# A fused gated linear attention and SiLU feed-forward: five masked scores split between ScalarE and VectorE, state updates spread over two engines, one pool for the inputs, and a new order of all work

## Chip, core and metric

The kernel runs on one core of one Trainium2 chip. The metric is the device time in microseconds (us) of one execution. Engines are named as in the profile: PE is TensorE (PEld its weight loads), DVE is VectorE, ACT is ScalarE, POOL is GpSimd, SP is SyncE, which only issues transfers here.

## What is computed

A recurrence over 768 positions for 4 x 8 heads of width 48, whose outputs go through a feed-forward block with SiLU (384 to 2048 to 384). Cut to what matters:

```python
f = 1.0 / (1.0 + np.exp(-f_logit))
for t in range(S):
    state = f[:, :, t, :, None] * state + np.einsum('bhd,bhe->bhde', k[:, :, t], v[:, :, t])
    y[:, :, t] = np.einsum('bhd,bhde->bhe', q[:, :, t], state)
x = y.transpose(0, 2, 1, 3).reshape(B * S, H * D)
h = x @ w_in
out = (h / (1.0 + np.exp(-h))) @ w_out
```

## The kernel before

The recurrence is computed in chunks of 128 positions. The logarithms of the gates are summed within a chunk by a matmul with a triangular matrix (`cs`); their exponentials `a` and `ia` scale q and k. Within a chunk the result is masked scores (q k^T, times a triangular mask) times v; across chunks a state of 48x48 per head is carried.

There are 24 chunks (4 batch rows, 6 chunks each), and the work goes by twelve pairs of chunks (`PAIRS`). Pairs 0 to 3 (form T) hold the first two chunks of one batch row, interleaved so that one load has both; pairs 4 to 11 (form N) hold the same chunk of two batch rows. A pair gives 256 columns for the feed-forward part.

Nothing schedules the work but a text, `PLAN`: one word per step, and every engine does its own steps in the order of the text. A word is `kind.pair.index:engine:buffers`; the engines are S (SP), A (ACT), V (DVE), G (POOL), P (PE). The steps, in the order of a chunk's life:

- `f`, `k`, `q`, `v`: loads. `E`, `L`: exponential and logarithm of the gate, on ACT. `cs`: the sum over the chunk, on PE. `a`, `ia`, `al`: exponentials of it, on ACT (`al` is the decay of a whole chunk).
- `qg`, `ki`: q and k times these, on DVE or POOL, into the tile `qk`. `tq` and `qkc`: transpose on PE and its copy, for pairs 0 to 3; `qkD`: the same as a transposing transfer on SP's queue, for the others.
- `sc`: scores on PE. `at`: scores from PSUM times the mask, on DVE, into `atm` (bf16). `vb`: v as bf16. `y`: masked scores times v, with the state's part (`yi` where that is a step of its own).
- `d`: k^T v on PE; `sd`: the state plus that; `su`: that times the decay, into the state `st`.
- `yc`, `yT`, `xc` (or `yD`, a transposing transfer): y as bf16, transposed, as input `xT` of the feed-forward part. `mi.P.j`: an eighth of its first product on PE (6 matmuls). `si`: SiLU on ACT. `mo.P.i.n`: a quarter of the second product for one chunk (4 matmuls). `oc`, `so`: copy and store of the result.
- `wi`, `wo`: a quarter each of w_in and w_out, by POOL's queue. `idle.C.N`: N matmuls of C columns whose result nobody reads; they keep PE working in the start.

Before, `at` is always one DVE instruction that reads PSUM:

```python
elif kind == "at":
    r = rest[2]
    mask = masks[i] if T else triu
    ENG[eng].tensor_mul(at("atm", P, i)[:, r], at(f"s{r}", P, i).rearrange("p (n c) -> p n c", c=C), mask[:, None, :].to_broadcast([C, NP, C]))
```

and `su` is always two POOL instructions, one for each half of the heads. Loads of f, k, q and v have buffers of their own (`SLOTS`: 4, 6, 6 and 6, of which the order uses 2, 2, 2 and 3), `E` writes into a buffer `e`. A step that needs a buffer waits until the last reader of the buffer's former content is done; what stands behind it on the same engine waits too.

Of the kernel before, what the change touches and what calls it, by code (L numbers as in the profile page):

```python
# [517 lines left out]
```

## Time and profile before

| what | value |
|---|---|
| median of three runs | 177.89 us (177.02 to 178.26) |
| the profiled execution | 177.35 us |
| its span, first to last instruction | 175.6 us |
| granted clock of PE | 1.0 |
| busy PE, ACT, DVE, POOL | 169.4, 129.8, 81.2, 61.2 us |
| DMA | 32.12 MB, 183 GB/s mean over the span |

The span is what the views of the profile show; 1.75 us of the profiled execution lie outside it. Rows of a view give an engine, the line of the kernel, the operation, output and inputs by tile name (`pb` is a PSUM bank of 512 fp32, `x` the exponentials, `qkTT` and `qkT` the transposed q and k), partitions x elements and type. In groups and in the timeline a matmul's duration includes the time it takes to drain, so that rows of PE overlap. A window's row has for each engine the busy time and the number of instructions, then PE's granted clock, the share of the DMA engines' time, and GB/s.

### The profile page before, as it was taken

Reading aid. Unit: us, or ns where it says so; the run is one execution under the profiler, and the core shown is the slowest. Engines: PE = TensorE matmul, PEld = TensorE weight load, DVE = VectorE, ACT = ScalarE, POOL = GpSimd, SP = SyncE. Lnnn points to the kernel's source line nnn. Section 1 sums busy time; section 2 is a strip of 40 time slices with the busy share of each in tenths; the row PEclk is TensorE's granted clock in tenths of the full one; section 3 lists DMA queues with packets and bytes.
Section 4 is the critical chain, followed back from the end, with each engine's and each line's share of the span. In section 5 each row is a group of like instructions: output and inputs, shape, how many; then the busy total and the mean of one; then the engine's idle time right before and its main releaser. Section 6 shows DMA issues by size and latency. Waiting matters only on the chain.

```text
span 175.6 us, 4754 instructions
## 1 busy us (share of the span) xinstructions
PE 169.4 (96%) x1927; PEld 125.2 (71%) x1930; DVE 81.2 (46%) x166; ACT 129.8 (74%) x239; POOL 61.2 (35%) x104
## 2 busy tenths in 40 slices
PE   6889999999999999999999999999999999999992
PEld 2446788666886788766787687686797676786872
DVE  7199760047786782125777165035770152520101
ACT  3968578952999989998489687999489575191630
POOL 6048393002473348400646324400461970000000
PEclk9999999999999999999999999999999999999999
DMA  5999999999998997999697797899967999223202
GB/s 146 320 325 265 211 216 201 188 182 240 232 172 164 210 208 158 228 183 217 128 230 166 143 236 158 205 188 231 225 128 183 193 191 230 54 61 118 90 4 90
DMA packets 110677, 32.12 MB, mean 183 GB/s; under 512 B 104096, under 2 KB 110528, under 8 KB 110656
## 3 DMA queue, kind: packets, MB, share of 16 engines
q1 hardware_dynamic: 106048, 27.76, 76.0%
q0 software_dynamic: 3936, 3.74, 11.9%
q10 hardware_dynamic: 672, 0.33, 0.6%
q8 instruction: 15, 0.25, 0.6%
q14 instruction: 6, 0.05, 0.1%
HBM read 25.17 MB, written 4.72 MB: 170 GB/s over the span
## 4 chain that ended last, share of the span: by engine, by line
PE 79%; ACT 11%; DVE 5%; DMA 2%; issue 2%
PE pb L286 35%; PE pb L249 29%; ACT x L317 3%; ACT hT L254 3%; PE pb L350 3%; ACT L485 2%; DVE qk L322 2%; DMA f<-in_f_logit_dram 2%; PE pb L362 2%; PE pb L366 2%; PE pb L346 1%; PE pb L312 1%; PE pb L383 1%; PE pb L374 1%; DVE atm L354 1%
## 5 line engine op out<-in xcount | busy, mean ns | idle before, releaser
L249 PE MATMUL pb<-xT,w_in_sb 128*128 128x256 bf16 x576 | 69.1, 272 | 0.3 <-ACT hT L254 0.2
L286 PE MATMUL pb<-w_out_sb,hT 128*128 128x384 bf16 (+2 forms) x400 | 68.6, 320 | 0.0
L249 PEld LDWEIGHTS <-w_in_sb 128*128 128x128 bf16 x576 | 54.8, 98 | 9.0 <-issue 0.8
L254 ACT ACTIVATE hT<-pb 128x512 bf16<-128x512 f32 x96 | 50.5, 611 | 10.9 <-PE pb L249 10.7
L286 PEld LDWEIGHTS <-hT 128*128 128x128 bf16 x400 | 37.2, 98 | 20.5 <-issue 0.2
L393 POOL TENSOR_TENSOR st<-sd,al 48x192 bf16<-48x192 f32 x40 | 21.4, 535 | 59.0 <-PE pb L362 33.4
L354 DVE TENSOR_TENSOR atm<-pb,triu 128x512 bf16<-128x512 f32 x32 | 20.1, 684 | 11.2 <-PE pb L350 6.6
L317 ACT ACTIVATE x<-pb 128x384 f32<-128x384 f32 x48 | 21.0, 501 | 5.4 <-PE pb L305 3.0
L485 ACT ACT_TABLE_LOAD x17 | 21.8, 1283 | 0.3
L184 DVE COPY ob<-pb 128x384 f32<-128x384 f32 (+1 forms) x11 | 5.7, 528 | 27.3 <-PE pb L286 27.3
L387 DVE TENSOR_TENSOR sd<-pb,st 128x384 f32<-128x384 f32 x16 | 8.8, 552 | 11.8 <-PE pb L383 10.3
L322 POOL TENSOR_TENSOR qk<-q,x 128x384 bf16<-128x384 f32 x11 | 10.9, 996 | 9.0 <-ACT x L317 6.1
L322 POOL TENSOR_TENSOR qk<-k,x 128x384 bf16<-128x384 f32 x11 | 11.8, 1081 | 5.7 <-ACT x L317 2.4
L182 ACT COPY ob<-pb 128x384 f32<-128x384 f32 (+1 forms) x14 | 6.7, 477 | 8.5 <-PE pb L286 8.1
L234 ACT ACTIVATE e<-f 128x768 f32<-128x768 f32 x12 | 10.1, 840 | 3.8 <-DMA f<-in_f_logit_dram 3.7
L322 DVE TENSOR_TENSOR qk<-q,x 128x384 bf16<-128x384 f32 x13 | 8.2, 648 | 7.2 <-ACT x L317 7.1
L354 DVE TENSOR_TENSOR atm<-pb,mask 128x512 bf16<-128x512 f32 x16 | 10.1, 684 | 1.6 <-issue 1.0
L436 PE MATMUL pb<-zero,triu 128*128 128x512 bf16 (+1 forms) x26 | 9.0, 449 | 1.4 <-POOL triu masks.py:66 1.4
L184 DVE CAST yb<-pb 128x384 bf16<-128x384 f32 x14 | 7.6, 554 | 5.1 <-PE pb L366 2.6
L184 DVE COPY qkTT<-pb 128x1024 bf16<-128x1024 bf16 x7 | 4.6, 683 | 11.0 <-PE pb L329 11.0
L322 DVE TENSOR_TENSOR qk<-k,x 128x384 bf16<-128x384 f32 x13 | 9.0, 707 | 1.0 <-DMA k<-in_k_dram 0.8
L184 POOL CAST vb<-v 128x384 bf16<-128x384 f32 x12 | 6.4, 535 | 8.0 <-DMA v<-in_v_dram 7.7
(71 smaller groups left out, 141.1 us busy)
## 6 DMA issues: line engine op xcount, KB each, us to landing
f<-in_f_logit_dram SPq DMA_DIRECT2D x11, 384.0 KB, 5.1
k<-in_k_dram SPq DMA_DIRECT2D x10, 384.0 KB, 5.5
q<-in_q_dram SPq DMA_DIRECT2D x10, 384.0 KB, 5.4
v<-in_v_dram SPq DMA_DIRECT2D x10, 384.0 KB, 4.9
out_dram<-ob SPq DMA_DIRECT2D x13, 192.0 KB, 2.1
w_in_sb<-in_moe_w_in_dram POOLq DMA_DIRECT2D x4, 384.0 KB, 8.6
w_out_sb<-in_moe_w_out_dram POOLq DMA_DIRECT2D x4, 384.0 KB, 10.5
out_dram<-ob SPq DMA_DIRECT2D x14, 96.0 KB, 3.3
```

What stands on the lines that cost most here:

```text
L184: ENG[eng].tensor_copy(dst, src)
L234: return nc.scalar.activation(e, at("f", P)[:, j * w:(j + 1) * w], AF.Exp, scale=-1.0)
L249: nc.tensor.matmul(h[:, i, cols], w_in_sb[:, kk, n * 128:(n + 1) * 128], at("xT", P)[:, kk, cols], start=(kk == 0), stop=(kk == KT - 1))
L254: return nc.scalar.activation(at("hT", P)[:, 2 * j:2 * j + 2, :], at("h", P, j).rearrange("p (n c) -> p n c", n=2), AF.Silu)
L286: nc.tensor.matmul(at("o" + key, P, i)[:, 0:cols.stop - cols.start], at("hT", P)[:, n, i * C:(i + 1) * C], w_out_sb[:, n, cols], start=(n ...
L317: nc.scalar.activation(at(kind, P, i).rearrange("p h d -> p (h d)"), at("cs", P, i)[:, 0:HD], AF.Exp, scale=1.0 if kind == "ia" else -1.0)
L322: ENG[eng].tensor_mul(at("qk", P, i)[:, j, :, 0:D], heads("qk"[j], P, i), at("ia" if j else "a", P, i))
L354: ENG[eng].tensor_mul(at("atm", P, i)[:, r], at(f"s{r}", P, i).rearrange("p (n c) -> p n c", c=C), mask[:, None, :].to_broadcast([C, NP, C]))
L387: nc.vector.tensor_add(at("sd", P, i), d_ps, prev_state(P, i))
L393: nc.gpsimd.tensor_mul(at("st", P, i)[lo:lo + D, :, r * D:(r + 1) * D], at("sd", P, i)[lo:lo + D, :, r * D:(r + 1) * D], al_of(P, i)[lo:lo ...
L436: nc.tensor.matmul(buf["pb", int(got)][:, 0:rest[0]], triu, zero[:, 0:rest[0]], start=True, stop=True, skip_group_check=True)
L485: nc.scalar.preload_act_table_set(turns[n])
```

## The change

1. Four masked scores of pairs 1 and 0 and one of pair 2 are split: ACT copies the scores from PSUM to `atm` as bf16 (`ax`), and DVE (or POOL, for pair 2) multiplies `atm` by the mask in place (`am`).
2. `su` may run on DVE: 12 of the 20 do, 8 stay on POOL.
3. f, k, q and v share one pool of input buffers (`inp`, of which the order uses 8), and `E` works in place.
4. The masks are built in fewer steps, partly on DVE; filler matmuls use the zero tile for both operands; the matmuls that give `al` its input (`on`) are a step of their own, which may follow later than `cs`.
5. `PLAN` is written anew from end to end. Among other things the second quarter of w_in (`wi.3`) is requested right behind the first (`wi.1`), and filler falls from 14080 to 10496 columns.

Otherwise the number of steps of each kind stays the same. By engine: `oc` on ACT 14 to 10 (DVE 11 to 15), `sd` on ACT 2 to 0, `vb` on ACT 6 to 9, `xc` on ACT 4 to 6, `qkc` on ACT 1 to 2; `ki` on POOL 11 to 14, `qg` on POOL 11 to 9.

```diff
-SLOTS = dict(f=4, k=6, q=6, v=6, e=2, lf=3, x=5, qk=5, vb=7, ...)
+SLOTS = dict(inp=24, lf=3, x=5, qk=5, vb=7, ...)
 PLAN = """
-f.1.0:S:0 f.1.1:A: E.1.0:A:0 L.1.0:A:0 idle.512.10::0 cs.1.1:P:0 f.0.0:S:1 E.0.0:A:1 k.1.0:S:0 L.0.0:A:1 idle.512.1::1 cs.1.0:P:1
+f.1.0:S:0 f.1.1:A: E.1.0:A: L.1.0:A:0 mk.0:G: mk.1:G: mv.0:V: idle.512.10::0 cs.1.0:P:0 f.0.0:S:1 E.0.0:A: idle.256.1::1 cs.1.1:P:1 k.1.0:S:2
...
+        if kind == "mv":
+            nc.vector.tensor_copy(tincl, triu)
+            for t in (tincl, tstrict):
+                nc.vector.memset(t[0:HC, HC:C], 0.0)
...
-            e = at("e", P)[:, j * w:(j + 1) * w]
+            e = at("f", P)[:, j * w:(j + 1) * w]
             if kind == "E":
-                return nc.scalar.activation(e, at("f", P)[:, j * w:(j + 1) * w], AF.Exp, scale=-1.0)
+                return nc.scalar.activation(e, e, AF.Exp, scale=-1.0)
...
+        elif kind == "ax":
+            nc.scalar.copy(at("atm", P, i)[:, rest[2]], at(f"s{rest[2]}", P, i).rearrange("p (n c) -> p n c", c=C))
+        elif kind == "am":
+            half = at("atm", P, i)[:, rest[2]]
+            ENG[eng].tensor_mul(half, half, (masks[i] if T else triu)[:, None, :].to_broadcast([C, NP, C]))
...
         elif kind == "su":
             for r in range(2):
                 lo = 64 * r
-                nc.gpsimd.tensor_mul(at("st", P, i)[lo:lo + D, :, r * D:(r + 1) * D], at("sd", P, i)[lo:lo + D, :, r * D:(r + 1) * D],
+                ENG[eng].tensor_mul(at("st", P, i)[lo:lo + D, :, r * D:(r + 1) * D], at("sd", P, i)[lo:lo + D, :, r * D:(r + 1) * D],
                                      al_of(P, i)[lo:lo + D, :, None].to_broadcast([D, NP, D]))
...
-                nc.tensor.matmul(buf["pb", int(got)][:, 0:rest[0]], triu, zero[:, 0:rest[0]], start=True, stop=True, skip_group_check=True)
+                nc.tensor.matmul(buf["pb", int(got)][:, 0:rest[0]], zero[:, 0:C], zero[:, 0:rest[0]], start=True, stop=True, skip_group_check=True)
...
-        loads = [t for t in plan if t[0] in SRC][:4]
-        for t in loads:
+        first = [t for t in plan if t[0] in SRC][:2]
+        first = [t for t in first if t[2] == "A" or t is first[0]]
+        for t in first:
             run(*t)
```

What the new order does shows in the engines' own rows. First ACT from the first exponential on, before and after (line and operation, output<-inputs; `e`, `f` and `inp` hold gates, `lf` their logarithms, `x` the four factors `a`, `ia` of pair 1, `pb` its sums):

```order
L234 ACTIVATE e_83<-f_61 128x768
L238 ACTIVATE lf_85<-e_83 128x8x2x48
L234 ACTIVATE e_84<-f_62 128x768
L238 ACTIVATE lf_86<-e_84 128x8x2x48
L317 ACTIVATE x_88<-pb_140 128x384
L317 ACTIVATE x_89<-pb_141 128x384
L317 ACTIVATE x_90<-pb_140 128x384
L317 ACTIVATE x_91<-pb_141 128x384
```

```order
L251 ACTIVATE inp_61<-inp_61 128x768
L255 ACTIVATE lf_85<-inp_61 128x8x2x48
L251 ACTIVATE inp_62<-inp_62 128x768
L340 ACTIVATE x_88<-pb_140 128x384
L340 ACTIVATE x_89<-pb_140 128x384
L340 ACTIVATE x_90<-pb_141 128x384
L340 ACTIVATE x_91<-pb_141 128x384
L255 ACTIVATE lf_86<-inp_62 128x8x2x48
L251 ACTIVATE inp_65<-inp_65 128x768
L255 ACTIVATE lf_85<-inp_65 128x8x2x48
```

The logarithm of pair 0's gates (`lf_86`) has moved from ahead of pair 1's four factors to behind them, with pair 2's gates right after it.

Second DVE between the masked scores of pair 1 and those of pair 0, before and after (`atm_111` and `atm_112` hold the masked scores of a pair's two chunks, `sd` and `st` the state):

```order
L354 TENSOR_TENSOR atm_111<-pb_141,mask_159 128x512
L354 TENSOR_TENSOR atm_111<-pb_144,mask_159 128x512
L354 TENSOR_TENSOR atm_112<-pb_147,mask_160 128x512
L354 TENSOR_TENSOR atm_112<-pb_141,mask_160 128x512
L322 TENSOR_TENSOR qk_93<-q_72,x_89 128x8x48
L322 TENSOR_TENSOR qk_94<-q_72,x_90 128x8x48
L184 CAST yb_115<-pb_141 128x384
L387 TENSOR_TENSOR sd_126<-pb_146,st_149 128x384
L184 COPY qkTT_110<-pb_143 128x16x64
L354 TENSOR_TENSOR atm_111<-pb_143,mask_160 128x512
```

```order
L382 TENSOR_TENSOR atm_111<-pb_145,mask_160 128x512
L382 TENSOR_TENSOR atm_112<-pb_146,mask_159 128x512
L387 TENSOR_TENSOR atm_111<-atm_111,mask_160 128x512
L382 TENSOR_TENSOR atm_112<-pb_147,mask_159 128x512
L182 COPY sd_126<-pb_146 128x384
L430 TENSOR_TENSOR st_149<-sd_126,al_129 48x4x48 x2
L424 TENSOR_TENSOR sd_127<-pb_143,st_149 128x384
L182 COPY qkTT_110<-pb_141 128x16x64
L182 COPY sd_126<-pb_146 128x384
L182 COPY xT_118<-pb_145 128x3x128
L382 TENSOR_TENSOR atm_111<-pb_143,mask_159 128x512
```

One of pair 1's four masked scores is now an `am` (its inputs are `atm` and a mask, none in PSUM), and the state's update `st_149` stands between two `sd` on DVE itself. Behind the last row come three `am` of pair 0 and the next update, `st_148`.

Third SP near the end, before and after (`qkT` and `xT` are written by transposing transfers, the other rows are loads and stores):

```order
L228 DMA q_72<-in_q_dram 128x16x48
L228 DMA k_66<-in_k_dram 128x16x48
L228 DMA k_65<-in_k_dram 128x16x48
L378 DMA_TRANSPOSE xT_119<-yb_116 128x3x128
L378 DMA_TRANSPOSE xT_119<-yb_115 128x3x128
L228 DMA q_71<-in_q_dram 128x16x48
L299 DMA out_dram<-ob_137 128x384
L337 DMA_TRANSPOSE qkT_108<-qk_96 128x8x128
L337 DMA_TRANSPOSE qkT_106<-qk_95 128x8x128
L228 DMA v_79<-in_v_dram 128x16x48
L228 DMA v_77<-in_v_dram 128x16x48
L337 DMA_TRANSPOSE qkT_107<-qk_94 128x8x128
```

```order
L415 DMA_TRANSPOSE xT_118<-yb_116 128x3x128
L415 DMA_TRANSPOSE xT_118<-yb_115 128x3x128
L321 DMA out_dram<-ob_134 64x384 x2
L245 DMA inp_65<-in_v_dram 128x16x48
L245 DMA inp_62<-in_q_dram 128x16x48
L245 DMA inp_67<-in_k_dram 128x16x48
L415 DMA_TRANSPOSE xT_119<-yb_115 128x3x128
L323 DMA out_dram<-ob_136 128x384
L415 DMA_TRANSPOSE xT_119<-yb_116 128x3x128
L366 DMA_TRANSPOSE qkT_105<-qk_93 128x8x128
L366 DMA_TRANSPOSE qkT_107<-qk_94 128x8x128
```

Before, q and k of pair 11 are loaded around the transposes `yD` of pair 8 (the first two `xT` rows), and its transposes `qkD` come ahead of those of `y.10`. Now all three loads of pair 11 (the rows with `inp`) follow `yD` of pair 8, and its two `qkD` follow both `yD` of pair 10 (the later `xT` rows).

248 lines of the change are left out of this document (130 added, 118 removed).

## Prediction, written before the changed kernel was run

> **What bounds the kernel now.** I read the busy totals and the row of TensorE in 40 slices first.
>
> ```profile
> span 175.6 us, 4754 instructions
> PE 169.4 (96%) x1927; PEld 125.2 (71%) x1930; DVE 81.2 (46%) x166; ACT 129.8 (74%) x239; POOL 61.2 (35%) x104
> ...
> PE   6889999999999999999999999999999999999992
> ```
>
> TensorE is busy for 96% of the span, and its only slices below nine are the first three and the last. A busy matmul row is not a full one, so the second view is one long window, which leaves out the start and the output's tail, and the third is what TensorE waited for.
>
> ```profile
> 22.50:172.50 150.00, 149.63 (x1639) 113.33 (x1635) 64.72 (x117) 114.75 (x209) 49.98 (x73) 1.00 0.88 174
> ```
> ```profile
> PE pb L436 <- POOL triu masks.py:66: 1.4, 1, 1.4
> PE pb L305 <- ACT lf L238: 0.5, 1, 0.5
> PE pb L329 <- ACT x L317: 0.4, 1, 0.4
> PE pb L329 <- DVE qk L322: 0.2, 1, 0.2
> PE pb L249 <- ACT hT L254: 0.2, 1, 0.2
> ```
>
> In 150 us TensorE lacks 0.37 us of work, at full clock (1.00). Of its 2.7 us of waits, 2.5 lie in the start. So from 22.5 us on nothing that is taken from ScalarE, VectorE or GpSimd can shorten the run; it can only lengthen it. What can be won lies ahead of 22.5 us, where TensorE also turns over filler matmuls:
>
> ```profile
> L436 PE MATMUL pb<-zero,triu 128*128 128x512 bf16 (+1 forms) x26 | 9.0, 449 | 1.4 <-POOL triu masks.py:66 1.4
> ```
>
> **The measure for the start.** Both orders put the same matmuls ahead of `y.0` (the masked-score product of pair 0) apart from filler, and the six steps behind it are the same: `yi.0.1`, `mi.1.6`, two `yT`, `mi.1.7`, `mi.0.3`. So the gain of the start is how much earlier `y.0` begins, less any wait just behind it. Before, these rows of the timeline lead there:
>
> ```profile
> 5.82 0.83 ACT L234 ACTIVATE e<-f 128x768 f32<-128x768 f32 x1
> 6.68 0.84 ACT L238 ACTIVATE lf<-e 128x768 bf16<-128x768 f32 x1
> 7.43 2.41 ACT L317 ACTIVATE x<-pb 128x384 f32<-128x384 f32 x6
> 12.10 0.84 ACT L234 ACTIVATE e<-f 128x768 f32<-128x768 f32 x1
> 15.24 0.58 PE L263 MATMUL pb<-vb,atm 64*128 64x48 bf16 x32
> 18.14 2.59 DVE L354 TENSOR_TENSOR atm<-pb,mask 128x512 bf16<-128x512 f32 x4 [0.52 <-PE pb L346]
> 20.08 1.08 POOL L393 TENSOR_TENSOR st<-sd,al 48x192 bf16<-48x192 f32 x2 [2.90 <-ACT sd L182]
> 20.83 0.57 PE L263 MATMUL pb<-vb,atm 64*128 64x48 bf16 x32
> 21.34 0.34 PE L362 MATMUL pb<-st,qkTT 128*128 128x96 bf16 x4
> ```
>
> `y.1` starts at 15.24 and `y.0` at 20.83, when the fourth masked score (18.14 + 2.59 = 20.73) is done.
>
> **The change, part by part.** *Filler.* 14080 columns become 10496. That alone is worth nothing: filler stands where TensorE would wait. It becomes a gain only if the waits shrink too.
>
> *ScalarE, first pair.* The gate factors of pair 1 now go ahead of `L.0`. They start 0.75 behind `E.0` (the distance from 6.68 to 7.43), at 6.57 instead of 7.43. Six of them take 2.41, the last about 0.5, so one passes every 0.38. Then `L.0` runs 8.1 to 8.95, `E.2` and `L.2` to 10.75 (two dependent steps of 0.84 to 0.88; their f is now the fifth load of the queue instead of the sixth, so I count it as landed; before, `E.2` began at 12.10), seven small steps to about 13.1 and the two casts of v to about 14.0 at 0.4 each. `d.1` starts then, and it stands ahead of `y.1` on TensorE; so `y.1` cannot start before 14.6, against 15.24.
>
> *Masks of pairs 1 and 0.* One masked score of pair 1 and three of pair 0 become a ScalarE copy and a bf16 product (`am`). The trace has neither operation. These rows are nearest:
>
> ```profile
> L354 DVE TENSOR_TENSOR atm<-pb,mask 128x512 bf16<-128x512 f32 x16 | 10.1, 684 | 1.6 <-issue 1.0 <-PE pb L346 0.5
> L254 ACT ACTIVATE hT<-pb 128x512 bf16<-128x512 f32 x96 | 50.5, 611 | 10.9 <-PE pb L249 10.7
> L184 DVE COPY qkTT<-pb 128x1024 bf16<-128x1024 bf16 x7 | 4.6, 683 | 11.0 <-PE pb L329 11.0
> L184 DVE COPY xT<-pb 128x384 bf16<-128x384 bf16 x11 | 3.8, 356 | 2.6 <-PE pb L374 2.3
> ```
>
> The copy moves what a silu moves, 128x512 from PSUM to bf16: 0.61. For `am` the upper bound is the masked score itself, 0.68; the lower, from the two bf16 copies on VectorE (0.356 for 384, 0.683 for 1024, so 0.51 ns per element), is 0.42. I take 0.42, since input and output are bf16 as in those. Four then save 4 x (0.68 - 0.42) = 1.0 us of VectorE, and pay 4 x 0.61 on ScalarE, beside VectorE's work on pair 0. The fifth `am` (pair 2, on GpSimd) lies in the stretch where TensorE has work from the feed-forward part; it costs nothing as long as that lasts.
>
> *State updates.* Twelve of twenty go from GpSimd to VectorE, four of them in the start. Bounds for two instructions: 1.08 as on GpSimd (20.08), or 0.55, half of a 384-element product each (the row of 23.45 below has 0.55 for one). I take 0.6. Here a new wait arises: `su.0.0` is queued behind the last `am` on VectorE, and `yi.0.1` waits for it. `y.0` covers 21.34 - 20.83 = 0.5, so TensorE waits 0.1 to 0.6; I take 0.2. Before, GpSimd had finished this at 21.16, under `y.0`.
>
> *What stands against it.* The new products have two inputs in SBUF, where a masked score has one in PSUM. This is how such a product fares beside GpSimd:
>
> ```profile
> 23.45 0.55 DVE L322 TENSOR_TENSOR qk<-q,x 128x384 bf16<-128x384 f32 x1
> 23.88 0.99 POOL L322 TENSOR_TENSOR qk<-q,x 128x384 bf16<-128x384 f32 x1
> 23.92 1.37 DVE L322 TENSOR_TENSOR qk<-k,x 128x384 bf16<-128x384 f32 x1
> ```
>
> Alone it takes 0.55; beside GpSimd's product it ends at 25.29, 0.42 behind GpSimd's end (24.87). It did not get on until GpSimd was through. [...] In the start `ki.0.1` and `qg.0.1` run on GpSimd from about 12.2 to 14.2 (`ia.0.1` is ready at 12.2; 0.99 to 1.08 each), and the `am` of pair 1 comes up at 13.4. It then ends at 14.6 instead of 13.8, the last masked score of pair 1 at 15.2, and `y.1` starts at 15.25, no earlier than before.
>
> *From y.1 to y.0.* The state chain follows on VectorE: `sd.1.0` 15.7, `su.1.0` 16.3, `sd.1.1` 16.8, the transposed copy (0.68) 17.45. Scores of pair 0 from 17.5; VectorE's one masked score and three `am`, fed by ScalarE every 0.5, end near 20.15, since GpSimd only issues weight requests there. So `y.0` starts at 20.2: 0.6 earlier. Without the block it would be 19.6 (1.2 earlier); with `am` at 0.68 and updates at 1.08 it would be 20.8 (nothing).
>
> *Weights.* w_in is asked for by GpSimd:
>
> ```profile
> 9.56 0.91 POOL L207 DMA_DIRECT2D w_in_sb<-in_moe_w_in_dram  x1
> 13.33 0.81 POOL L207 DMA_DIRECT2D w_in_sb<-in_moe_w_in_dram  x1
> ...
> DMA to landing us min/median/max: 6.5/8.6/10.2
> ```
>
> The first piece still goes out near 9.5 (behind `ki.1.1`), the second near 10.4 instead of 13.33. Even at the longest landing, 10.2, that is 20.6, about when `mi.1.6` wants it. Nothing is lost there, and nothing won.
>
> *Later on.* The net move is about 4 us onto ScalarE and 11 off GpSimd, all of it inside the 150 us that TensorE fills. ScalarE has 114.75 of those 150, so the cover is 35 us; if a step were late there, each microsecond would count in full. I take nothing.
>
> **Sum.** 0.6 - 0.2 = 0.4 us off the profiled execution's 177.35 (span 175.6 and 1.75 around it): 176.95. The median of the runs is 177.89, 0.54 above that execution, which gives 177.5 the same way. I say 177.1.
>
> **Rivals.** *The block does not bite* (GpSimd's products fall between VectorE's): `y.0` at 19.6 and 0.1 of wait give 1.1, and the 0.37 that TensorE lacks later may go too: 177.35 - 1.5 = 175.9. For it: GpSimd loses masks and state updates ahead of this place. Against it: the row of 23.92.
>
> *The last pair comes late.* The inputs now share one pool of buffers, so k of pair 11 is asked for only when v of pair 10 is cast, and its two transposes are queued on SP behind those of `y.10`:
>
> ```profile
> L337 SPq DMA_TRANSPOSE qkT<-qk x16: 1239/1568/2590, 48.6 to 143.9; - x16
> ...
> DMA to landing us min/median/max: 3.2/4.1/5.2
> ```
> ```profile
> L378 SPq DMA_TRANSPOSE xT<-yb x9: 1178/1198/1726, 96.2 to 155.5; - x9
> ```
>
> ```profile
> 145.59 4.55 PE pb L286 x28
> ```
> ```profile
> 150.08 0.62 PE L350 MATMUL pb<-qkT 48*128 48x128 bf16 x16
> ```
> ```profile
> 10.00:15.00 5.00, 4.59 (x76) 2.55 (x76) 4.95 (x11) 3.10 (x8) 3.03 (x5) 1.00 1.20 287
> ...
> 140.00:160.00 20.00, 20.00 (x216) 15.29 (x214) 7.26 (x13) 10.85 (x22) 3.70 (x7) 1.00 0.64 146
> ```
>
> From the end of `y.10.0` to the scores `sc.11.1` TensorE has 10.0 us of work: eight output blocks and six input blocks at 0.65 (28 matmuls, seven blocks, in 4.55), the scores `sc.11.0` at 0.55 and `y.10.1` at 0.37. In that time SP must pass: the cast of y, 0.75; `yD`, 1.2; an output, 0.6; `yD`, 1.2; `qkD.11.0`, 1.57; and `qkD.11.1` must land, 4.1: 9.4 us. That is 0.6 to spare. At the maxima (1.73, 1.73, 2.59, 5.2) it is 12.6, and TensorE waits 2.6: 177.1 + 2.6 = 179.7, slower. It decides from 10.0 us on. Before, the last transpose went out at 143.9 and the scores came at 150.08, so there was room. For it: 0.6 is thin, and other early loads have short windows too. Against it: past 140 us the DMA share is 0.64, against 1.20 in the start.
>
> *The change brings no time*: `am` at 0.68 and updates at 1.08 leave `y.0` at 20.8, and the time at 177.9.
>
> **Chances.** The forecast has 0.38, no change 0.05, the faster rival 0.24, the late last pair (or the same wait at another of the shared buffers) 0.33. About 1% is what a measurement of this kernel can tell from no change: 176.1 to 179.7. Faster takes the faster rival's 0.24 and 0.01 of the forecast, slower the 0.33, the rest is 0.42. The likeliest case by itself runs from 176.1 to 178.1, by the bounds of `y.0` (1.2 or nothing). The range reaches to the rivals on both sides, with 0.5 us for the spread of the runs at the fast end and a microsecond more of waits at the other: 175.4 to 180.6.
>
> **What would show it.** In the profile after: `y.1` near 15.25 and `y.0` near 20.2; the bf16 product at 0.42 alone and over 0.7 beside GpSimd; a wait of TensorE at the first state product; from there TensorE as full as before. The forecast is wrong if TensorE shows waits of over a microsecond beyond 22 us (the scores of pair 11 first of all), or if `y.0` starts before 19.6 or after 20.8.

## The result, and the profile after

The changed kernel takes 183.27 us (median of six runs, 181.98 to 185.60) against 177.57 for the kernel before on the same chip: a ratio of 1.030, 95% interval 1.026 to 1.035. It is 3% slower. The prediction, 177.1 in 175.4 to 180.6, missed on the slow side. The profiled execution took 182.55 us.

The page of the changed kernel, answering the rows shown of before:

```profile
span 180.8 us, 4747 instructions
...
PE 169.6 (94%) x1924; PEld 126.1 (70%) x1925; DVE 88.1 (49%) x192; ACT 133.3 (74%) x244; POOL 47.6 (26%) x73
...
PE   7668989999999999999999999999979999999993
...
PEclk9979999999999999999999999999999999999999
```

PE's row has gaps in the first slices and a 7 in slice 30 (131 to 136 us), and the granted clock (`PEclk`) falls to 0.7 in slice 3. What PE waited for, in the whole execution:

```profile
PE pb L329 <- ACT lf L255: 2.8, 2, 1.7
PE pb L378 <- DVE atm L382: 1.4, 1, 1.4
...
PE pb L354 <- DVE qk L347: 1.0, 2, 0.7
PE pb L399 <- DVE st L430: 0.8, 1, 0.8
```

And the long window of the prediction (150.00, 149.63 before), then the two stretches before and while the clock is low:

```profile
22.50:172.50 150.00, 147.62 (x1646) 112.01 (x1644) 73.34 (x143) 115.22 (x209) 36.93 (x52) 1.00 0.90 174
7.45:10.86 3.41, 1.24 (x19) 0.79 (x18) 1.67 (x4) 1.44 (x3) 0.48 (x1) 1.00 1.17 325
10.86:14.27 3.41, 3.19 (x23) 1.91 (x22) 1.11 (x3) 3.13 (x8) 2.18 (x3) 0.50 1.11 303
```

The rows of the timeline that answer those of the prediction:

```profile
8.59 0.62 PE L354 MATMUL pb<-ident,qk 128*128 128x128 bf16 x8 [0.70 <-DVE qk L347]
9.04 0.34 PE L276 MATMUL pb<-halves,lf 128*128 128x2 bf16 x8
9.42 0.87 ACT L340 ACTIVATE x<-pb 128x384 f32<-128x384 f32 x2 [1.98 <-PE pb L276]
10.18 0.84 ACT L255 ACTIVATE lf<-inp 128x768 bf16<-128x768 f32 x1
11.08 0.48 PE L329 MATMUL pb<-lf,tincl 128*128 128x384 bf16 x1 [1.69 <-ACT lf L255]
16.97 0.76 DVE L387 TENSOR_TENSOR atm<-atm,mask 128x512 bf16<-128x512 bf16 x1
18.39 0.58 PE L287 MATMUL pb<-vb,atm 64*128 64x48 bf16 x32 [0.42 <-DVE atm L382]
23.36 1.42 DVE L430 TENSOR_TENSOR st<-sd,al 48x192 bf16<-48x192 f32 x2
23.44 0.57 PE L287 MATMUL pb<-vb,atm 64*128 64x48 bf16 x32
23.52 1.04 POOL L347 TENSOR_TENSOR qk<-inp,x 128x384 bf16<-128x384 f32 x1 [0.56 <-issue]
24.83 0.33 PE L399 MATMUL pb<-st,qkTT 128*128 128x96 bf16 x4 [0.82 <-DVE st L430]
```

`y.1` begins at 18.39 (15.24 before), `y.0` at 23.44 (20.83), `yi.0.1` at 24.83 (21.34). From `yi.0.1` to the last matmul it is 152.7 us (150.9). So of 5.3 us between the two traces 3.5 are lost by `yi.0.1` and 1.8 behind it. The first three rows explain about half of the start: the eight small matmuls of the second row, `on.1`, stand behind the transposes of the first and end near 9.4, and ScalarE, which does nothing meanwhile, has waited 1.98 us for them. `L.0` is late by that, and TensorE then waits 1.69 us for it (the fifth row), in the stretch ahead of the half clock. The experiments part the two: at full clock, with `on.1` still late, `y.1` comes at 16.78 to 16.89 (e2, e3), and with `on.1` early at 15.12 (e1). So of the 3.15 us that `y.1` is late, some 1.5 go to the half clock and 1.7 to the late sums.

This table has every kernel that ran. "Clock" is the lowest mean granted clock among its runs; the times of the steps and "rest" (`yi.0.1` to the begin of the last matmul) come from the one traced execution. The ratio leaves out executions over 1.5% above the fastest of their kernel, the median does not, so the ratio counts where they differ (e5, e6, e7, e11); the traces of e5, e6 and e11 are of such longer executions.

| kernel | median us | ratio to before | clock | y.1 | y.0 | yi.0.1 | rest |
|---|---|---|---|---|---|---|---|
| before | 177.3 to 177.6 | 1 | 0.997 | 15.24 | 20.83 | 21.34 | 150.9 |
| changed | 183.27 | 1.030 (1.026 to 1.035) | 0.979 | 18.39 | 23.44 | 24.83 | 152.7 |
| e1 sums early | 184.10 | 1.039 (1.035 to 1.043) | 0.971 | 15.12 | 23.66 | 24.17 | 153.4 |
| e2 filler in gap | 181.49 | 1.023 (1.020 to 1.025) | 0.997 | 16.89 | 21.94 | 23.34 | 153.5 |
| e3 ki.2.1 on DVE | 181.29 | 1.021 (1.017 to 1.024) | 0.990 | 16.78 | 21.83 | 22.52 | 154.0 |
| e4 transposes earlier | 184.73 | 1.043 (1.039 to 1.047) | 0.981 | 17.55 | 22.69 | 24.08 | 157.1 |
| e5 e1, w_in apart | 182.77 | 1.020 (1.015 to 1.026) | 0.972 | 15.01 | 24.79 | 25.34 | 156.1 |
| e6 three mended | 181.62 | 1.018 (1.013 to 1.022) | 0.981 | 15.15 | 24.84 | 25.49 | 153.8 |
| e7 e6, masks whole | 181.30 | 1.013 (1.010 to 1.017) | 0.981 | 15.46 | 21.76 | 22.39 | 152.6 |
| e8 before, w_in pair | 177.29 | 0.999 (0.998 to 1.001) | 0.997 | 15.17 | 20.76 | 21.27 | 151.3 |
| e9 e6, casts behind | 181.65 | 1.022 (1.018 to 1.027) | 1.000 | 15.18 | 21.73 | 22.82 | 153.2 |
| e10 before, less filler | 178.81 | 1.008 (1.005 to 1.012) | 0.981 | 15.55 | 22.20 | 22.71 | 151.0 |
| e11 e9, masks whole | 181.76 | 1.019 (1.014 to 1.025) | 1.000 | 15.32 | 22.27 | 22.89 | 154.8 |
| e12 e6, filler in gap | 181.84 | 1.023 (1.019 to 1.027) | 0.998 | 15.08 | 22.20 | 22.90 | 153.8 |
| e13 e9, k early | 180.48 | 1.016 (1.012 to 1.019) | 0.998 | 14.95 | 21.50 | 22.59 | 151.2 |
| e14 before, one split | 177.44 | 1.001 (0.999 to 1.002) | 0.997 | 15.28 | 20.86 | 21.48 | 151.6 |

### The profile page after: what moved, and what is told of

It is laid out like the page before. It is cut to its first block, busy times and chain, and to the rows that moved or that the text cites. A ratio compares the mean times of both kernels' runs of the same rounds, so it can differ in the third digit from the quotient of the medians.

```text
span 180.8 us, 4747 instructions
## 1 busy us (share of the span) xinstructions
PE 169.6 (94%) x1924; PEld 126.1 (70%) x1925; DVE 88.1 (49%) x192; ACT 133.3 (74%) x244; POOL 47.6 (26%) x73
## 4 chain that ended last, share of the span: by engine, by line
PE 77%; DVE 7%; ACT 7%; DMA 5%; issue 2%; SPq 1%; DVEq 0%
PE pb L266 31%; PE pb L310 31%; DMA inp<-in_q_dram 3%; PE pb L378 2%; PE pb L399 2%; DVE qk L347 2%; PE pb L403 2%; PE pb L354 2%; DVE atm L382 2%; DMA inp<-in_v_dram 2%; DVE st L430 2%; ACT hT L271 1%; ACT L509 1%; ACT x L340 1%; PE pb L411 1%
## 5 line engine op out<-in xcount | busy, mean ns | idle before, releaser
L347 POOL TENSOR_TENSOR qk<-inp,x 128x384 bf16<-128x384 f32 x23 | 23.3, 1019 | 56.8 <-ACT x L340 23.8
L182 DVE COPY ob<-pb 128x384 f32<-128x384 f32 (+1 forms) x15 | 7.8, 535 | 28.4 <-PE pb L310 25.1
L347 DVE TENSOR_TENSOR qk<-inp,x 128x384 bf16<-128x384 f32 x25 | 14.7, 608 | 8.9 <-ACT x L340 7.3
L182 POOL CAST vb<-inp 128x384 bf16<-128x384 f32 x11 | 5.4, 506 | 25.6 <-DMA inp<-in_v_dram 25.5
L251 ACT ACTIVATE inp<-inp 128x768 f32<-128x768 f32 x12 | 10.1, 843 | 2.1 <-DMA inp<-in_f_logit_dram 2.1
L430 POOL TENSOR_TENSOR st<-sd,al 48x192 bf16<-48x192 f32 x16 | 8.1, 507 | 10.7 <-PE pb L399 5.4
L430 DVE TENSOR_TENSOR st<-sd,al 48x192 bf16<-48x192 f32 x24 | 9.1, 381 | 0.5
L180 ACT CAST yb<-pb 128x384 bf16<-128x384 f32 x10 | 4.8, 484 | 5.3 <-PE pb L403 3.9
L473 PE MATMUL pb<-zero 128*128 128x512 bf16 (+1 forms) x23 | 7.4, 423 | 1.2 <-DVE halves L499 1.2
L382 DVE TENSOR_TENSOR atm<-pb,mask 128x512 bf16<-128x512 f32 x11 | 7.0, 680 | 2.8 <-PE pb L374 2.8
```

Source lines behind the costliest of these rows:

```text
L180: nc.scalar.copy(dst, src)
L182: ENG[eng].tensor_copy(dst, src)
L251: return nc.scalar.activation(e, e, AF.Exp, scale=-1.0)
L347: ENG[eng].tensor_mul(at("qk", P, i)[:, j, :, 0:D], heads("qk"[j], P, i), at("ia" if j else "a", P, i))
L430: ENG[eng].tensor_mul(at("st", P, i)[lo:lo + D, :, r * D:(r + 1) * D], at("sd", P, i)[lo:lo + D, :, r * D:(r + 1) * D], al_of(P, i)[lo:lo ...
```

## The experiments

### e1: the sums of pair 1 ahead of the transposes

```diff
-cs.1.1:P:1 k.1.0:S:2 ... tq.1.0:P:0 on.1:P: a.1.1:A:2
+cs.1.1:P:1 on.1:P: k.1.0:S:2 ... tq.1.0:P:0 a.1.1:A:2
```

> The eight small matmuls that sum the gate logs of pair 1 (on.1) stand ahead of the transposes tq.1.0 instead of behind them; nothing else is changed. They write the PSUM bank that the gate factors a.1.1 and ia.1.1 read. Theory A (in the changed kernel ScalarE waits 1.98 us behind on.1, which waits behind tq.1.0 for q, and that wait runs through L.0, E.2, L.2 and the casts of v to y.1): a.1.1 starts near 7.5 instead of 9.42, L.0 near 8.3 instead of 10.18, y.1 about 1.5 to 2 us before 18.39, and the time falls by 1.5 to 2.0 us, to 181.3 to 181.8. Theory B (VectorE, with its products of two SBUF inputs beside GpSimd's, sets y.1 and y.0): L.0 is earlier in the same way, but y.0 stays within 0.4 us of 23.44 and the time within 0.4 us of 183.3. Under either, TensorE's gap at 9.2 shrinks from 1.83 us to under 1; if the granted clock then stays at 1.00 between 11 and 14, the gap was what brought it down.

Timeline of e1:

```profile
6.75 1.64 ACT L340 ACTIVATE x<-pb 128x384 f32<-128x384 f32 x4
...
7.90 2.38 SPq L245 DMA_DIRECT2D inp<-in_v_dram  x2
...
8.25 0.86 ACT L255 ACTIVATE lf<-inp 128x768 bf16<-128x768 f32 x1
...
9.41 1.72 POOL L211 DMA_DIRECT2D w_in_sb<-in_moe_w_in_dram  x2
...
12.23 1.95 POOL L347 TENSOR_TENSOR qk<-inp,x 128x384 bf16<-128x384 f32 x2 [1.10 <-ACT x L340]
...
13.42 1.05 DVE L387 TENSOR_TENSOR atm<-atm,mask 128x512 bf16<-128x512 bf16 x1
...
17.50 0.51 ACT L180 CAST vb<-inp 128x384 bf16<-128x384 f32 x1 [2.77 <-DMA inp<-in_v_dram]
...
18.45 0.34 PE L411 MATMUL pb<-ident,yb 128*128 128x128 bf16 x3 [1.78 <-ACT yb L180]
```

The first half of theory A holds: all four gate factors run in one go, `L.0` starts at 8.25, and `y.1` at 15.12, 3.3 us sooner. That is more than forecast because PE's gap at 9.4 is gone too and the clock is full until 20.21. But the kernel is not faster. ScalarE reaches the cast of v of pair 0 (`vb.0.0`) before v is there, stands 2.77 us, and the cast of y of pair 1 is queued behind it; PE waits 1.78 for that, and the clock is half from 20.21 to 23.62. The gained time was handed to the next late thing, a load.

Why that load is late shows in the two rows of requests. Of the two loads of v the second, v of pair 0, goes out at 9.91 only: it shares an input buffer with q of pair 1, which VectorE reads until 9.88. The first piece of w_in goes out ahead of it, at 9.41, and v lands at 17.48. In the changed kernel v goes out at 10.53, ahead of w_in at 11.32, and lands at 13.90. All sixteen traces go this way: asked for ahead of w_in, v of pair 0 landed at 13.9 to 14.2 (nine traces), behind it at 16.1 to 17.7 (seven). No run changed this order alone.

### e2: filler in PE's gap

```diff
-L.0.0:A:1 cs.0.0:P:2
+L.0.0:A:1 idle.512.7::5 cs.0.0:P:2
```

> Seven more filler matmuls of 512 columns (1.5 us at full clock) fill TensorE's gap at 9.3 to 11.1, ahead of the gate sums of pair 0; the late sums on.1 and all else stay. Theory A: L.0 stays at 10.18 and ScalarE's chain with it. Granted clock: 1.00 from 11 to 14 instead of 0.50, if the idle gap brought it down. If the half clock is what makes the start late (theory C), y.1 comes about 1 us earlier (cs.0, tq.1.1, on.0 and cs.2.1 cost 1.0 us more than at full clock) and the time falls to about 182.3. By theory A TensorE's half clock hides under ScalarE's chain: y.1 moves by less than 0.4 us and the time stays at 183.0 to 183.4.

```profile
16.89 0.58 PE L287 MATMUL pb<-vb,atm 64*128 64x48 bf16 x32 [0.53 <-DVE atm L382]
```

`L.0` stayed at 10.17, and the clock was 0.997 or more in all six runs, against five of six at 0.991 or less, down to 0.979, in the changed kernel. The time fell by 1.8 us (1.3 by the ratios): theory C, not A, and more than C had forecast. So the half clock did not hide under ScalarE; `y.1` came at 16.89 instead of 18.39. One thing does not fit: the one run of the changed kernel with a clock of 1.00 took 183.64, no less than the others. It has no trace, so this stays open.

### e3: a key product taken off GpSimd

```diff
-ki.2.1:G:
+ki.2.1:V:
```

> The gated key product of pair 2, second half (ki.2.1) goes from GpSimd to VectorE, behind su.0.1. In the changed kernel it runs on GpSimd at 23.52 to 24.56, and the state update su.0.0 on VectorE beside it takes 1.42 instead of 0.72, while TensorE waits 0.8 for it ahead of yi.0.1. Theory A (a VectorE product with two SBUF inputs does not get on beside a GpSimd product): the two instructions of su.0.0 take about 0.72 together, TensorE's wait falls from 0.8 to about 0.1, yi.0.1 starts near 24.1 instead of 24.83 and the time falls by 0.6 to 0.7 us, to 182.6. Rival (su.0.0 is slow by itself, or something else ends late there): 1.42 stays and the time stays at 183.3.

```profile
21.75 0.71 DVE L430 TENSOR_TENSOR st<-sd,al 48x192 bf16<-48x192 f32 x2
...
22.52 0.33 PE L399 MATMUL pb<-st,qkTT 128*128 128x96 bf16 x4
```

Without the product beside it the update `su.0.0` takes 0.71 instead of 1.42, and `yi.0.1` follows `y.0` by 0.69 instead of 1.39. This is theory A to the tenth of a microsecond. The time fell by 2.0 us (1.7 by the ratios), and the trace shows only 0.7 of that to be this edit. The rest is in part luck: nothing ahead of 21 us was edited and PE's wait of 1.69 us is still there, yet the clock did not fall in the traced run, and it fell in two of six runs here against five of six of the changed kernel. Why the rest of the program is 1.3 longer in this trace (154.0) is open.

### e4: the transposes of pair 8 earlier

```diff
-yD.9.1:S: mo.7.0.2:P: so.4.1:S: ... k.10.0:S:4 ... qkD.8.1:S:1 ... qkD.8.0:S:3
+yD.9.1:S: qkD.8.1:S:1 qkD.8.0:S:3 mo.7.0.2:P: so.4.1:S: ... k.10.0:S:4
```

> The two DMA transposes of pair 8 (qkD.8.1, qkD.8.0) are asked for right behind the transpose of y of pair 9, ahead of an output row block and of k of pair 10, instead of behind them; nothing else. In the changed kernel qkD.8.0 goes out at 130.63 and the scores sc.8.0 wait for it until 135.64. Theory A (that wait is the place in SP's queue): both go out 1.1 us earlier, the wait of 1.36 falls to 0.3 or less and the time falls by 1.0 to 1.4 us, to 182.0 to 182.3. Rival (the transposes are held by the transfers in flight and not by their place): the issue takes as much longer as it starts earlier, the scores come at the same time and the time stays at 183.3; or k of pair 10 comes late in its place and TensorE waits behind 136.

The place in the changed kernel, in its timeline:

```profile
133.88 0.40 PE L378 MATMUL pb<-qkT 48*128 48x128 bf16 x8
135.64 0.22 PEld L378 LDWEIGHTS <-qkT 48*128 48x128 bf16 x8 [1.54 <-DMA qkT<-qk]
135.64 0.40 PE L378 MATMUL pb<-qkT 48*128 48x128 bf16 x8 [1.36 <-DVE atm L382]
```

The list of waits names `atm`; the weight load beside it shows that the transfer came last. In e4 that wait is gone, and a worse one is there:

```profile
132.89 0.56 DVE L182 COPY ob<-pb 128x384 f32<-128x384 f32 x1 [5.82 <-DMA out_dram<-ob]
...
133.50 0.33 PE L420 MATMUL pb<-vb,qk 128*128 128x96 bf16 x4 [2.10 <-DVE ob L182]
```

The store `so.4.1`, now behind the transposes, frees the output buffer that `oc.7.0` needs; VectorE stood 5.8 us, PE 2.1, and behind that gap the clock was half from 134.49 to 137.90. What was moved back on SP mattered more than what was moved ahead.

### e5 and e6: w_in apart, and three places mended together

```diff
-wi.1:G: wi.3:G: ki.0.1:G:3 qg.0.1:G:
+wi.1:G: ki.0.1:G:3 qg.0.1:G: wi.3:G:
```

> The early sums of the first experiment, and the second w_in piece (wi.3) asked for behind qg.0.1 on GpSimd instead of back to back with the first. In the first experiment both pieces went out at 9.41 and 10.35 and the ninth load (v of pair 0) landed at 17.5 to 18.4; ScalarE waited 2.77 us for it in vb.0.0, with the cast of y of pair 1 queued behind, TensorE stood still for 1.94 us at 16.5, and the granted clock was half from 19.9 to 23.1. In the kernel before, with one piece on the way, the ninth load landed at 15.99. Theory A (the back-to-back pieces share the transfers with v of pair 0, and this was what kept the first experiment from gaining): v lands near 16.0 to 16.5, ScalarE's wait falls to 1.3 us or less, TensorE's gap at 16.5 to under 0.7, y.0 starts near 21.5 instead of 23.66, the granted clock stays at 1.00 in the start, and the time falls from 184.1 to 181 to 182. Rival (v is late because of its own place in SP's queue, behind q and k of pair 0): v lands past 17, and the time stays at 183 to 184.

> The kernel of e5 with two more places mended: ki.2.1 on VectorE, as in the third experiment, and the two transposes of pair 8 ahead of the output block and of k of pair 10, as in the fourth, but with the output buffers of oc.7.0 and oc.9.0 and of the blocks behind them swapped, so that oc.7.0 does not wait for the output block that now goes out later (in the fourth experiment VectorE stood still for it for 5.8 us and TensorE for 2.1). Theory A (the late start, the state update beside GpSimd's product and the late transposes are the three places where the changed kernel lost its time): against e5 0.7 us less ahead of yi.0.1 and 1.0 to 1.4 less at the scores sc.8.0; 179 to 180 us, within 1.5% of the kernel before. Rival (the time goes from place to place, since a late transfer or engine is behind each wait): under 0.8 us less than e5.

e6 adds to e5 the edits of e3 and e4, with output buffers 1 and 2 swapped from `oc.7.0` on.

Moving the second piece away did not bring v of pair 0 forward: it landed at 17.6 in e5 and 17.7 in e6 (17.5 in e1), past 17 as the rival in e5 had it. It was still asked for behind the first piece (9.78 and 9.28 in e5), and ScalarE waited 3.04 and 2.94 us there. PE's wait remained, 2.0 and 1.9 us, and the clock was half for 6.8 us after it in both traces. By the ratios e5 gained 1.9% on e1. That goes with the clock (0.991 or less in all runs of e1, 0.997 or more in two of the three of e5 that count), and the traces do not show why; e6 gained nothing certain on e5 (1.018 against 1.020). Near 136 us PE of e6 waited 1.5 us again, now behind k of pair 10 (VectorE had waited 1.63 for it, with the masked scores queued behind). The rival, that time goes from place to place, holds.

### e7 and e11: the masks made whole again

```diff
-ax.1.1.0:A: am.1.1.0:V: ... ax.0.0.0:A: am.0.0.0:V: ax.0.1.0:A:1 am.0.1.0:V: ax.0.1.1:A: am.0.1.1:V:
+at.1.1.0:V: ... at.0.0.0:V: at.0.1.0:V:1 at.0.1.1:V:
```

> The kernel of e6 with four of the five split masks made whole again: one masked score of pair 1 and three of pair 0 are one VectorE product from PSUM, as in the kernel before, instead of a ScalarE copy and a product of two bf16 tiles. Each takes 0.68 on VectorE instead of 0.41 to 0.45 alone, and 0.76 to 1.05 beside a GpSimd product. Theory A (for pair 0 the split saves VectorE 0.25 a score, and costs ScalarE 0.6 a score, which is free there): y.0 comes 0.5 to 0.8 us later than in e6 and the time rises by as much. Rival (the split saves nothing, since ScalarE's copies come one every 0.6 and the split product of pair 1 is held by GpSimd): y.1 comes 0.3 to 0.5 earlier, y.0 at the same time within 0.3, and the time is equal to that of e6 or up to 0.5 lower.

> The kernel of e9 with four of the five split masks made whole again, as e7 was to e6. Between e7 and e6 the undisturbed runs were equal (179.2 to 180.4 against 179.8). Theory A (the split is worth 0.5 to 0.8 us once nothing else holds pair 0): 0.5 to 0.8 us slower than e9. Rival (the split moves work without a gain: what VectorE saves, the copies on ScalarE give back): within 0.3 us of e9.

The traces of e6 and e7 differ in clock and tell nothing on this; e9 and e11 do. In e9 `y.0` comes 0.54 earlier than in e11, as theory A has it, but `yi.0.1` only 0.07 (22.82 and 22.89): the state update behind the `am` sets that. The intervals of the ratios overlap in both pairs, and e7 is if anything the faster. Neither a gain nor a cost of the split shows here, within intervals of about half a per cent.

### e8: back-to-back w_in in the kernel before

```diff
-wi.1:G: al.1:A:0 ... sd.1.1:V:0 wi.3:G:
+wi.1:G: wi.3:G: al.1:A:0 ... sd.1.1:V:0
```

> The kernel before, with the second w_in piece asked for right behind the first (GpSimd issues it at about 10.5 instead of 13.33); nothing else. Theory A (two pieces back to back push back the loads that are asked for after them): the ninth load, v of pair 0, lands near 17.5 to 18.5 instead of 15.99. In this kernel its casts stand behind other work (the first one on ScalarE ran after 18), so y.0 moves by 0 to 0.8 us from 20.83 and the time by 0 to 0.8 from 177.3. Rival (the transfers have room): v lands at 16 and the time stays within 0.3; then the lateness of v in the first experiment comes from elsewhere.

From the request to the landing of v of pair 0 (asked for at 9.0), before and in e8, then of q of pair 2 (asked for at 10.5):

```profile
DMA to landing us min/median/max: 4.9/4.9/4.9
DMA to landing us min/median/max: 5.2/5.2/5.2
```
```profile
DMA to landing us min/median/max: 7.8/7.8/7.8
DMA to landing us min/median/max: 12.7/12.7/12.7
```

The rival holds: v landed at 14.16 instead of 13.86, and the time is the same (0.999, interval 0.998 to 1.001). The 15.99 of the expectation is a miscount: it is the time at which nine whole loads' worth of bytes had come by SP's queue, but half of the first load goes by ScalarE's queue, so that the bytes of v are complete half a load sooner. What the pair does push back are the next loads, q and k of pair 2, from 18.32 to 23.18 and from 22.54 to 25.87. VectorE waited 2.89 us for that k, but TensorE had other work.

### e9: the late casts behind the casts of y

```diff
-vb.0.0:A:2 ... yc.1.0:A:0 vb.0.1:A:0 ... yT.1.0:P:7 d.0:P:6,4 sd.0.0:V:0 yT.1.1:P:5 sc.0.0:P:1,3 xc.1.0:A:0 ... mi.1.2:P:5
+... yc.1.0:A:0 ... yT.1.0:P:7 yT.1.1:P:5 sc.0.0:P:1,3 xc.1.0:A:0 vb.0.0:A:2 vb.0.1:A:3 ... mi.1.2:P:5 d.0:P:6,4 sd.0.0:V:0
```

> The kernel of e6 with the casts of v of pair 0 (vb.0.0, vb.0.1) moved on ScalarE from ahead of the casts of y of pair 1 to behind the first copy of its transposes (xc.1.0), and d.0, which needs them, moved on TensorE behind the first input block of pair 1 (mi.1.2). In e6 ScalarE stood for 2.94 us at vb.0.0, whose input's last packet landed at 17.68, with the cast of y queued behind, TensorE stood for 2.1 us at 16.5, and the granted clock was half from 18.6 to 25. Theory A (the order on ScalarE puts the late load in the path, and the gap brings the clock down): TensorE's gap at 16.5 falls to under 0.5, the granted clock stays at 1.00 in all runs, y.0 starts near 21.3 instead of 24.4, and the time falls to 178 to 179. Rival (pair 0 is late by the load itself): the gap moves to d.0 and the time stays at 179.7 or more.

```profile
17.29 0.34 PE L411 MATMUL pb<-ident,yb 128*128 128x128 bf16 x3 [0.40 <-ACT yb L180]
...
21.73 0.81 PE L287 MATMUL pb<-vb,atm 64*128 64x48 bf16 x32 [0.18 <-ACT atm L384]
```

PE's wait fell from 1.9 to 0.40 us, the clock is 1.00 in all six runs, and `y.0` starts at 21.73. In this trace v happened to land early, at 13.93; e11 and e13, where it landed at 16.1, have the same 0.40, so the order on ScalarE did it. That is half of theory A: the time did not follow. The trace has 0.9 us of waits near 93 us and 0.3 near 142 that earlier traces had in part or elsewhere; the other microsecond by which its rest is longer than before (153.2 against 150.9) is not accounted for.

### e10: the kernel before with less filler

Nine filler matmuls between 9 and 15 us left out, for instance:

```diff
-qg.1.0:V: idle.512.3::5 tq.1.0:P:1
+qg.1.0:V: tq.1.0:P:1
```

> The kernel before without nine of its filler matmuls between 9 and 15 us (4096 columns; the changed kernel has 3584 fewer than the kernel before); no other instruction is moved. Theory A (TensorE's clock is brought down to half when the start has too little work for it, whatever the cause): TensorE has gaps of 0.5 to 1.2 us between 9.4 and 15, the granted clock is below 1.00 in some or all runs, and the time rises by 0.5 to 3 us over 177.3. Rival (filler stands where TensorE would wait anyway, and is worth nothing): the clock stays at 1.00 and the time within 0.3 us of 177.3.

Three windows of e10 (PE busy is the second number, the clock the third from the end), then the rows of its timeline with `y.0` and `yi.0.1`:

```profile
8.14:11.56 3.42, 2.40 (x44) 1.68 (x42) 3.22 (x7) 2.24 (x6) 1.40 (x2) 1.00 1.17 325
11.56:14.97 3.41, 2.04 (x51) 1.33 (x46) 3.36 (x7) 2.53 (x6) 2.47 (x4) 1.00 1.22 266
14.97:18.38 3.41, 3.41 (x54) 2.77 (x53) 2.26 (x6) 2.76 (x7) 2.26 (x4) 0.50 1.18 280
```

```profile
22.20 0.57 PE L263 MATMUL pb<-vb,atm 64*128 64x48 bf16 x32
22.71 0.34 PE L362 MATMUL pb<-st,qkTT 128*128 128x96 bf16 x4
```

The clock was 0.99 or less in all six runs, and half for 3.41 us in the trace; `y.0` is 1.37 later, the rest of the program is as before (151.0 against 150.9), and the median is 1.5 us higher. Matmuls whose result nobody reads were worth 0.8% of the time.

### e12: filler in the second gap

```diff
-yc.1.1:A:1 yT.1.0:P:7
+yc.1.1:A:1 idle.512.8::4 yT.1.0:P:7
```

> The kernel of e6 with eight filler matmuls of 512 columns (1.7 us at full clock) in TensorE's gap at 16.5, ahead of the transposes of y of pair 1; ScalarE's order and the late v stay. Theory A (the half clock of e5 and e6 comes from that gap): the granted clock is 0.997 or more in all runs, they lie within 1 us of each other, and the median falls from 181.6 to 179.5 to 180. Rival (the clock falls for another reason): the clock falls below 0.99 in as many runs as in e6 (three of six), and the time stays at 181 to 182.

The clock stayed at 0.998 or more in all six runs (e6: three of six at 0.991 or less), so the gap was its cause. But the median did not fall (1.023 against 1.018): e6's runs at full clock took 179.8 to 181.7, e12's 180.5 to 182.1. Here filler took away the executions at half clock and did nothing for the others.

### e13: k of pair 10 in a buffer of its own

```diff
-q.10.0:S:1 ... k.10.0:S:4
+q.10.0:S:1 k.10.0:S:10 ...
```

> The kernel of e9 with k of pair 10 in an input buffer of its own (the shared pool has unused ones) and asked for right behind q of pair 10, ahead of an output block, the transposes of y of pair 9 and those of pair 8. In the kernels with the transposes moved ahead of it, the products of pair 10 waited for k on VectorE by 1.0 to 2.2 us and on GpSimd by 5.6 to 7.8, and TensorE stood still near 134 us for 0.2 to 2.2 us; in the changed kernel itself, where k goes out first, the transposes are late instead and TensorE waits 1.4 us for the scores. Theory A (near 134 us one place of SP's queue holds three things that are all wanted at once, and the shared buffer of k, free only when v of pair 8 is cast, forces k behind): k lands before it is wanted, TensorE's gap near 134 us is under 0.4, the runs lie closer together than 179.75 to 182.24, and the median falls from 181.65 to 180 to 181. Rival (another transfer becomes late in its place, those of y of pair 9 first of all): the gap moves to the input blocks of pair 9 near 129 and the time stays at 181.2 or more.

One stretch near the end, in the changed kernel and in e13:

```profile
130.00:146.00 16.00, 14.64 (x160) 10.99 (x157) 6.23 (x13) 10.50 (x17) 3.97 (x7) 1.00 0.99 170
```

```profile
130.00:146.00 16.00, 16.00 (x182) 12.43 (x180) 8.28 (x16) 11.16 (x20) 3.60 (x7) 1.00 0.84 172
```

Theory A: PE lacks nothing there any more, and the rest is 151.2 us, 0.3 from the kernel before. The median fell by 1.2 us, to 180.48, and the ratio from 1.022 to 1.016, with intervals that barely overlap. The buffer and the place in the queue were changed together, so which of the two was needed is not shown. The traced execution took 179.12, the others 180.3 to 181.0 and one 184.2; what held those has no trace.

### e14: one split mask in the kernel before

```diff
-xc.1.1:A: sd.0.0:A:1 su.0.0:G:0 mi.1.2:P:7 mi.1.3:P:3 at.0.1.1:V:
+xc.1.1:A: ax.0.1.1:A: sd.0.0:A:1 su.0.0:G:0 mi.1.2:P:7 mi.1.3:P:3 am.0.1.1:V:
```

> The kernel before with one of the masked scores of pair 0, the last (at.0.1.1), split into a ScalarE copy (behind xc.1.1, where ScalarE is idle for 0.4 us) and a product of two bf16 tiles on VectorE; nothing else. It is the changed kernel's headline edit alone, at the place where the kernel before waits for VectorE: y.0 starts at 20.83 when this score is done at 20.73. Theory A (the split saves 0.25 us of VectorE): the product takes 0.41 to 0.45 instead of 0.65, y.0 starts near 20.6 and the time falls by 0.2 to 0.3 us to 177.05 or so. Rival (GpSimd's state update su.0.0, two products from 20.1 to 21.2, runs beside it and holds the product with two SBUF inputs; the copy also pushes sd.0.0 and su.0.0 back by 0.2 to 0.6): the product takes 0.8 to 1.3, y.0 starts at 21.0 to 21.4, yi.0.1 waits for su.0.0, and the time rises by 0.2 to 0.8 us.

```profile
18.97 0.69 ACT L356 CAST atm<-pb 128x512 bf16<-128x512 f32 x1
...
19.45 1.49 PE L249 MATMUL pb<-xT,w_in_sb 128*128 128x256 bf16 x12
...
20.07 0.41 DVE L359 TENSOR_TENSOR atm<-atm,mask 128x512 bf16<-128x512 bf16 x1
20.13 1.30 POOL L398 TENSOR_TENSOR st<-sd,al 48x192 bf16<-48x192 f32 x2 [2.92 <-ACT sd L182]
20.86 0.58 PE L263 MATMUL pb<-vb,atm 64*128 64x48 bf16 x32
```

The product takes 0.41 and is done at 20.48, 0.25 before the whole score was, yet `y.0` starts at 20.86: PE was busy with two input blocks until then. The time is the same (1.001, interval 0.999 to 1.002). GpSimd's pair started 0.06 behind the product and took 1.30 instead of 1.08: here GpSimd paid.

No version beat the kernel before.

## Why the prediction was wrong, step by step

- **What bounds the kernel.** Right that from 22.5 us on nothing could be gained and all could be lost; the chance given to a loss there was too small. Wrong in the start: `y.0` at 20.83 was read as VectorE's, since the last score ended at 20.73. e14 shows that PE itself was full up to that moment. Two engines ended within 0.1 us, and only one was looked at.
- **ScalarE, first pair: the step that failed.** "The gate factors of pair 1 now go ahead of `L.0`", with one passing every 0.38. Only the first two ran so (6.59); the third began at 9.42. The last two read the PSUM bank into which the sums `on.1` are written; those stood behind the transposes `tq.1.0`, and these waited for q, whose load ended near 7.9. `L.0` came at 10.18 instead of 8.1, and that alone makes `y.1` 16.8 to 16.9 instead of 15.25 (e2, e3); the half clock, which the next item is about, makes it 18.39. e1 moved only the sums and had `L.0` at 8.25 and `y.1` at 15.12, so the rest of this step was sized well.
- **Filler "alone is worth nothing".** The second step that failed, by about 1.5 us: e10 in the kernel before, and 1.3 to 1.8 by e2 in the changed one, where the 3584 columns of e2 are just those that the change had taken out. The prediction had no term for the granted clock.
- **The bf16 product.** Right: 0.41 alone, 0.76 and 1.05 beside GpSimd, and held by it where foreseen. The copy took 0.59 (0.61 predicted). It did not matter (e7, e11, e14).
- **From `y.1` to `y.0`.** 4.95 us were forecast, and 5.05 are there in the changed kernel, e2 and e3. But they hold only while `y.1` is late. With `y.1` near 15 it takes 8.5 us in e1 and still 6.55 in e9 and e13, since v of pair 0, or its casts in their later place, come last. The forecast had no step for v of pair 0. No run of the changed order has `y.1` near 15, v asked for ahead of w_in and the casts in their first place, so whether the 0.6 us of the forecast can be had stays open.
- **State updates.** Two take 0.71 alone (0.6 predicted), but 1.42 beside `ki.2.1`, which was looked for at the masks and not here; PE waited 0.82 instead of 0.2. e3 shows it.
- **Weights.** "Nothing is lost there, and nothing won": right, but by luck. In the changed kernel v of pair 0 goes out ahead of w_in because the late sums hold up w_in's request as well (11.32 instead of 9.41 in e1). There, with the sums early, w_in goes first, and v lands 3.6 us later.
- **Later on.** "I take nothing"; 1.8 us were lost, 1.4 of them at one transpose on SP. The rival of the late last pair had the mechanism, named at pair 11; it came at pair 8. e4 shows that the order on SP makes it, and e13 that it goes away when k of pair 10 has a buffer of its own and is asked for earlier. The same sharing of buffers delays v of pair 0 in the start (e1).

With all these places mended (e13) the trace is 1.25 us behind the kernel before at `yi.0.1` and 0.3 behind it after; its median is 3.2 behind. The cause of the difference between that trace and the median is open.

## What to carry to other kernels

Before pricing a reordered chain, look for what is written into the same buffer by a third engine: a tiny instruction in the wrong place of another queue can hold the chain (here eight matmuls of two columns, 2 us). Where a shared queue is full, the instruction that is pushed back deserves as much thought as the one that is pulled ahead (in e4 a store put behind two transposes on SP, for which VectorE stood 5.8 us). When loads share buffers, ask which request waits for a buffer, and which other transfer then goes out first (in e1 w_in at 9.41, ahead of v at 9.91). Filler in a start was not free to cut (nine matmuls fewer in e10: the clock at 0.99 or less in all six runs, the median 1.5 us higher): count what is left in each stretch of a few microseconds, not only the waits.

## What the runs showed of the hardware

In the clock record of the changed kernel's trace the granted clock is 1.00 or 0.50. The first record of 1.00 begins at 4.03 us; filler matmuls of 512 columns start 0.43 us apart ahead of it and 0.22 behind it. The clock falls to 0.50 at 10.86 and is back at 1.00 at 14.27, 6.83 and 10.24 us after 4.03. The half clock lasts 3.41 us there, in e1, in e10 and at either place in e4 (from 11.61 and 134.49), and 6.8 us in the start of e5 and e6.

TensorE's busy time in the 3.41 us ahead of a fall was 1.24 us in the changed kernel, 1.76 in e1 (the second row below), 1.34 and 1.31 in e4, 1.55 in the start of e5 and of e6, and 2.04 in e10. The clock stayed at 1.00 after 1.87 us busy in e6 (the first row), 2.05 in the changed kernel (133.73 to 137.14) and 2.13 in e3 (9.72 to 13.13). Busy time alone does not tell: e6 kept its clock after less of it than e10, which lost its own. Nor does the length of a wait: e10 lost its clock with no wait of TensorE over 0.84 us between 9 us and the fall. What else counts was not shown. The same wait of 1.69 us fell into one such stretch in the changed kernel (1.24 us busy) and was cut in two in e3 (2.44 and 2.13), whose clock stayed at 1.00.

```profile
134.50:137.91 3.41, 1.87 (x26) 1.11 (x24) 1.77 (x4) 1.40 (x3) 1.16 (x1) 1.00 0.62 123
```

```profile
16.79:20.21 3.42, 1.76 (x48) 1.20 (x52) 1.73 (x5) 2.71 (x8) 2.50 (x4) 1.00 1.19 224
20.21:23.62 3.41, 3.41 (x29) 1.97 (x22) 2.28 (x6) 1.81 (x4) 0.00 (x0) 0.50 1.21 207
```

(The first is e6, the other two are e1, before the fall and in it.)
